# A weight's sign set by the two-slope rectifier, and the last output products of blocks 1 to 4 issued behind the next block's first projections

## The chip, the core and the metric

The kernel runs on one core of a Trainium2 chip. The metric is the time of one execution on the device in microseconds; less is better. The engines that matter are TensorE (PE in the profile, with its weight loads as PEld), VectorE (DVE), ScalarE (ACT), GpSimd (POOL) and SyncE (SP), whose queue issues nearly all transfers between DRAM and on-chip memory.

## What is computed

A causal attention over a window of 64 positions, then a gated MLP with an RMS norm in front of it, then a second MLP. Cut to its core:

```
scores = (q @ k.T) / 8, masked to 0 <= pos_q - pos_k < 64      # 4 x 8 heads, 576 positions, 64 wide
x  = softmax(scores) @ v                                        # rearranged to 2304 tokens x 512
xn = x / sqrt(mean(x*x) + 1e-6) * rms_g
g  = xn @ w_gate                                                # 512 x 1536
x  = (silu(g) * (xn @ w_val)) @ w_out                           # 1536 x 512
h  = x @ w_in2                                                  # 512 x 2048
y  = (h * sigmoid(1.702 * h)) @ w_out2                          # 2048 x 512
```

The MLP weights come as 64-bit floating-point numbers and are needed with more precision than TensorE's fast format holds. Each is turned on the core into two parts, a high one and a remainder, and so is each activation; a product is three matmul terms (high by high, high by remainder, remainder by high).

## The kernel before

The 2304 tokens are six blocks (0 to 5) of 384. The gated MLP runs in two passes over all blocks, six chunks f of 128 hidden units in each pass; the second MLP follows, again over six blocks. The attention of a block is three windows of 128 queries (m = 0 to 17 in all). Windows 0 to 2 are done ahead of everything; the others are woven into pass 0, one block ahead of the block that uses them, so that window 5 is the last that block 1 needs.

**One chunk** (the loop over f): twelve 128x384 matmuls into `psg` (the gate projection), ACT takes the tanh (L623) and DVE makes the gate from it (L626), which frees psg; twelve matmuls into `psv`, DVE multiplies (L630), ACT rounds to `ah` (L633), DVE takes the remainder `al` (L634). Then `emit_O` adds the products of the chunk before with `w_out` into four accumulators acc, again twelve matmuls. psg and psv have one PSUM bank each, so the next psg waits for this chunk's L626 and the next psv for its L630. Behind the last chunk a block has an emit_O without a partner; then the four accumulators are halved into `x2s` tiles (L666 on DVE, L668 on ACT), which have two buffers, and stored (L669).

**The input of a block** is split into `xh` (L423 on ACT, L421 on DVE) and `xl` (L425). A sum of squares on PE (`ps_r`), a power on POOL (L398) and a scaling (L409) stand ahead of that.

**One window of attention**: transposes of k and q, 32 score products `ps_s`, a masked reduction on DVE (L309), the exponential on ACT (L321), a division (L331 to L333), transposes `ps_t` copied out by ACT (L252), 32 value products `ps_v`. The loads of a later window's v wait until an earlier one's has been used.

**A weight step** (`w_step`, L147 on) works on 1024 64-bit words for each partition, as two 32-bit halves `lo` and `hi`: ACT scales `hi` (L163) and `lo` (L164), DVE shifts the exponent bits (L165), sets the sign bit back (L166), and adds `lo` (L169); half a step later ACT rounds (L144) and DVE takes the remainder (L145). There are 34 steps, nine of them in block 0.

**What sets the order.** In pass 0 from block 1 on, the PE instructions stand in program order, and the attention is called at ticks (`score_at`); one tick is one matmul of a projection or of emit_O. PE's order in block 0, and that of the other engines everywhere, is set by a scheduler that models the engines' times when the kernel is built. Between the end of the attention and the second MLP the tile `xr` brings back the first result (L450).

Of the kernel before, what the change touches and what calls it, by code (L numbers as in the profile page):

```python
# [8 lines left out]
F32 = mybir.dt.float32  # L9
F32R = mybir.dt.float32r  # L10
I32 = mybir.dt.int32
U32 = mybir.dt.uint32
AF = mybir.ActivationFunctionType
ALU = mybir.AluOpType
# [8 lines left out]
def window_attention__gated_mlp__mlp_kernel(  # L23
# [13 lines left out]
    nc = tc.nc  # L37
# [4 lines left out]
    KC = DM // 128  # L42
# [6 lines left out]
    TB = 384  # L49
# [8 lines left out]
    stp = ctx.enter_context(tc.tile_pool(name="stp", bufs=3))  # L58
    dram = ctx.enter_context(tc.tile_pool(name="dram", bufs=1, space=bass.MemoryType.DRAM))
    acc_p = ctx.enter_context(tc.tile_pool(name="acc", bufs=1, space=PSUM))  # L60
# [88 lines left out]
    def w_step(limit):  # L149
# [12 lines left out]
        with after(hold[0]):  # L162
            nc.scalar.mul(hi.bitcast(F32), hi.bitcast(F32), 2.0 ** -112)  # L163
            nc.scalar.activation(lo, lo.bitcast(U32), AF.Copy, scale=2.0 ** -29)  # L164
        nc.vector.tensor_scalar(m.bitcast(U32), hi.bitcast(U32), 3, None, ALU.logical_shift_left)  # L165
        nc.vector.scalar_tensor_tensor(  # L166
            m.bitcast(U32), hi.bitcast(U32), 0x80000000, m.bitcast(U32), ALU.bitwise_and, ALU.bitwise_or
        )
# [322 lines left out]
    score_at = [220, 268, 316, 364, 433, 502, 572, 642, 712, 784, 856, 928, 1000]  # L491
# [36 lines left out]
    if True:  # L528
# [49 lines left out]
        T = TB  # L578
        for ps_i in range(2):
            f_lo, f_hi = ps_i * FH, (ps_i + 1) * FH  # L580
            for j in range(NB):
                end = j + 1 == NB
                pinned[0] = ps_i == 0 and j > 0
                acc = [acc_p.tile([128, 512], F32, tag=f"acc{c}", name=f"acc{c}") for c in range(KC)]

                def emit_O(f, ah, al):
# [30 lines left out]
                for f in range(f_lo, f_hi):  # L617
# [24 lines left out]
                    extras(f, 1)  # L642
                    if pend is not None:
                        emit_O(*pend)
# [14 lines left out]
                emit_O(*pend)  # L659
                d = dram.tile([128, KC, TB], F32, name=f"o{ps_i}_{j}", tag=f"o{ps_i}_{j}")  # L660
                for c in range(KC):
                    st = stp.tile([128, TB], F32, tag="os", name="x2s", bufs=2)
                    if ps_i:
                        nc.vector.scalar_tensor_tensor(st, acc[c][:, :T], 0.5, part[:, c, :], ALU.mult, ALU.add)
                    elif c % 2:
                        nc.vector.tensor_scalar(st, acc[c][:, :T], 0.5, None, ALU.mult)  # L666
                    else:
                        nc.scalar.mul(st, acc[c][:, :T], 0.5)  # L668
                    nc.sync.dma_start(out=d[:, c, :], in_=st)  # L669
                (x2d if ps_i else od)[j] = d  # L670
# [86 lines left out]
```

## Time and profile before

| | us |
|---|---|
| median of three runs | 1009.71 |
| range of the runs | 1008.48 to 1009.97 |
| the profiled execution | 1009.22 |
| its span in the profile | 1007.4 |
| PE busy | 976.3 (97%) |
| DVE busy | 514.3 (51%) |
| ACT busy | 407.9 (40%) |

The profiled execution takes 1.8 us more than its span, and lies 0.5 us under the median of the runs. PE is busy nearly always. The stages by time: preparation to 36 us, block 0 to about 100, blocks 1 to 4 with boundaries at about 160, 218, 273 and 329, block 5 to 368, pass 1 to 591, the second MLP to the end.

### The profile page before, as it was taken

The numbers are of one execution on the slowest core, as the hardware profiler recorded it, in microseconds if no ns is written. First come the engines' busy times: TensorE is split into PE (matmuls) and PEld (weight loads), VectorE is DVE, ScalarE is ACT, GpSimd is POOL, SyncE is SP. The second block draws the span as 40 slices with busy tenths as digits, with TensorE's granted clock in tenths as the row PEclk, the third lists the DMA queues.
The fourth block names the chain that finished last, engine by engine and source line by source line (L and its number), as shares of the span: only waits on it lengthen the run. The fifth ranks groups of instructions, "written<-read, shape, count | busy, mean of one in ns | idle before, by whom it ended". The sixth has DMA issues, their size and how long they took to land.

```text
span 1007.4 us, 15580 instructions
## 1 busy us (share of the span) xinstructions
PE 976.3 (97%) x6218; PEld 913.0 (91%) x6218; DVE 514.3 (51%) x1132; ACT 407.9 (40%) x884; POOL 12.6 (1%) x39
## 2 busy tenths in 40 slices
PE   8888998999999999999999999999999999999997
PEld 7888898989988999999999998998999989989996
DVE  5797666576765555564543787242322322322222
ACT  7786655565553333333322464232222322322222
POOL 2000000000000000000000000000000000000000
PEclk9899999999999999999999999999999999999999
DMA  9867455354433431342330441010010100000000
GB/s 225 241 183 198 123 115 159 84 158 116 120 85 122 146 105 43 136 132 88 136 122 15 161 149 57 1 63 1 5 59 1 53 11 1 32 1 1 32 1 32
DMA packets 113321, 88.44 MB, mean 88 GB/s; under 512 B 77664, under 2 KB 104288, under 8 KB 113248
## 3 DMA queue, kind: packets, MB, share of 16 engines
q1 hardware_dynamic: 112720, 87.44, 29.4%
q8 instruction: 49, 0.80, 0.3%
q14 instruction: 24, 0.20, 0.1%
q10 hardware_dynamic: 528, 0.00, 0.0%
HBM read 68.55 MB, written 18.87 MB: 87 GB/s over the span
## 4 chain that ended last, share of the span: by engine, by line
PE 84%; DVE 6%; DMA 4%; ACT 3%; SPq 1%; issue 1%; POOL 0%; ACTq 0%; DVEq 0%
PE acc L684 20%; PE psh L91 20%; PE psg L91 13%; PE psv L91 13%; PE acc L91 12%; PE ps_v L91 1%; PE ps_t L91 1%; SPq L225 1%; PE ps_s L91 1%; DMA st<-in_moe_w_val_dram 1%; PE ps_r L91 1%; DMA o<-x2s 1%; ACT p L321 1%; DVE m L166 1%; DVE xraw L409 1%
## 5 line engine op out<-in xcount | busy, mean ns | idle before, releaser
L700 DVE TENSOR_TENSOR a<-a,psh 128x384 f32<-128x384 f32 x96 | 53.0, 553 | 202.5 <-ACT a L699 202.5
L91 PE MATMUL psh<-x2h,w 128*128 128x384 f32 x768 | 153.2, 339 | 0.2 <-DVE a L700 0.2
L684 PE MATMUL acc<-w,gh 128*128 128x512 f32 x576 | 152.8, 397 | 0.0
L91 PEld LDWEIGHTS psh<-x2h,w 128*128 128x128 f32 x768 | 137.2, 188 | 3.4 <-DVE a L700 0.6
L699 ACT ACTIVATE a<-psh 128x384 f32<-128x384 f32 x96 | 47.2, 492 | 220.5 <-PE psh L91 217.5
L684 PEld LDWEIGHTS acc<-w,gh 128*128 128x128 f32 x576 | 107.0, 188 | 18.5
L91 PE MATMUL acc<-ah,w 128*128 128x384 f32 x576 | 117.2, 341 | 2.5 <-ACT ah L633 2.5
L91 PEld LDWEIGHTS acc<-ah,w 128*128 128x128 f32 x576 | 101.5, 188 | 3.9 <-ACT ah L633 3.2
L91 PE MATMUL psh<-x2l,w 128*128 128x384 f32 x384 | 86.2, 338 | 0.0
L684 PE MATMUL acc<-w,gl 128*128 128x512 f32 x288 | 85.1, 396 | 0.0
L626 DVE SCALAR_TENSOR_TENSOR a<-a,psg 128x384 f32<-128x384 f32 x72 | 39.7, 551 | 88.1 <-ACT a L623 88.1
L704 DVE TENSOR_TENSOR gl<-a,gh 128x384 fp32r<-128x384 f32 x96 | 53.4, 557 | 50.5 <-ACT gh L703 42.7
L623 ACT ACTIVATE a<-psg 128x384 f32<-128x384 f32 x72 | 35.2, 489 | 104.4 <-PE psg L91 104.4
L91 PEld LDWEIGHTS psh<-x2l,w 128*128 128x128 f32 x384 | 69.9, 188 | 5.9
L703 ACT CAST gh<-a 128x384 fp32r<-128x384 f32 x96 | 49.3, 513 | 62.6 <-DVE a L700 49.7
L91 PE MATMUL psg<-xh,w 128*128 128x384 f32 x288 | 66.0, 360 | 8.8 <-DVE a L626 6.2
L633 ACT CAST ah<-a 128x384 fp32r<-128x384 f32 x72 | 37.0, 513 | 75.7 <-DVE a L630 75.5
L684 PEld LDWEIGHTS acc<-w,gl 128*128 128x128 f32 x288 | 54.2, 189 | 12.5
L91 PE MATMUL psv<-xh,w 128*128 128x384 f32 x288 | 64.4, 352 | 0.3 <-DVE a L630 0.3
L91 PE MATMUL acc<-al,w 128*128 128x384 f32 x288 | 63.9, 341 | 0.7 <-DVE al L634 0.7
L91 PEld LDWEIGHTS psg<-xh,w 128*128 128x128 f32 x288 | 52.3, 196 | 13.0 <-DVE a L626 7.3
L321 ACT ACTIVATE p<-p,sm 128x128 f32<-128x128 f32 x128 | 49.7, 393 | 25.5 <-DVE sm L309 25.4
(106 smaller groups left out, 1418.8 us busy)
## 6 DMA issues: line engine op xcount, KB each, us to landing
st<-in_moe_w_out_dram SPq DMA_DIRECT2D x28, 512.0 KB, 4.4
o<-x2s SPq DMA_DIRECT2D x48, 192.0 KB, 2.7
st<-in_moe_w_in_dram SPq DMA_DIRECT2D x16, 512.0 KB, 4.5
st<-in_moe_w_gate_dram SPq DMA_DIRECT2D x12, 512.0 KB, 4.4
st<-in_moe_w_val_dram SPq DMA_DIRECT2D x12, 512.0 KB, 5.5
qkv<-in_v_dram SPq DMA_DIRECT2D x20, 256.0 KB, 3.9
x<-xraw SPq DMA_DIRECT2D x6, 768.0 KB, 3.4
xr<-x SPq DMA_DIRECT2D x6, 768.0 KB, 4.1
```

The source lines that it names most:

```text
L91: ins = op(*args, **kw)
L166: nc.vector.scalar_tensor_tensor(m.bitcast(U32), hi.bitcast(U32), 0x80000000, m.bitcast(U32), ALU.bitwise_and, ALU.bitwise_or)
L225: nc.sync.dma_start(out=t[off:off + n], in_=src[b, :, s:s + n, :].rearrange("h s d -> s h d"))
L321: last_exp[0] = nc.scalar.activation(p[e][:, hp, :], p[e][:, hp, :], AF.Exp, bias=sm[:, 0, i:i + 1], scale=-1.0, accum_out=sm[:, 1, i:i + ...
L623: tanh = nc.scalar.activation(a, psg[:, :T], AF.Tanh, scale=0.5).ins
L626: nc.vector.scalar_tensor_tensor(a, a, 1.0, psg[:, :T], ALU.add, ALU.mult)
L633: ah_ins = nc.scalar.copy(ah, a).ins
L684: nc.tensor.matmul(acc[c], (gh, gh, gl)[pi][:, c * 128:(c + 1) * 128], w[:, (0, 1, 0)[pi], :], start=(f == 0 and pi == 0), stop=(f == NF2 ...
L699: nc.scalar.activation(a[:, :T], psh[:, :T], AF.Sigmoid, scale=1.702)
L700: nc.vector.tensor_tensor(a[:, :T], a[:, :T], psh[:, :T], ALU.mult)
L703: nc.scalar.copy(gh[:, :T], a[:, :T])
L704: nc.vector.tensor_tensor(gl[:, :T], a[:, :T], gh[:, :T].bitcast(F32), ALU.subtract)
```

## The change

Two things change. In a weight step ACT's multiplication by 2^-112 becomes the two-slope rectifier `Prelu`, with a scale of 2^16 and a slope of 2^-32 for negative numbers: a positive number comes out multiplied by 2^16, a negative one by 2^-16, so that a bit of the exponent tells the sign, and the shift by three puts that bit where the sign belongs. The DVE instruction that set the sign (L166 before) is gone. And in pass 0 the last emit_O of blocks 1 to 4, with the halving and the stores behind it, is kept in `late` and called in the next block after the first psg and psv. The next block's accumulators are made after that. The fifth tick is 3 earlier, the sixth 7, and all from the seventh on 12.

```diff
@@ -160,12 +160,9 @@
         else:
             m = tmp.tile([128, 1024], I32, tag="tmp", name="m")
         with after(hold[0]):
-            nc.scalar.mul(hi.bitcast(F32), hi.bitcast(F32), 2.0 ** -112)
+            nc.scalar.activation(hi.bitcast(F32), hi.bitcast(F32), AF.Prelu, scale=2.0 ** 16, alpha=2.0 ** -32)
             nc.scalar.activation(lo, lo.bitcast(U32), AF.Copy, scale=2.0 ** -29)
         nc.vector.tensor_scalar(m.bitcast(U32), hi.bitcast(U32), 3, None, ALU.logical_shift_left)
-        nc.vector.scalar_tensor_tensor(
-            m.bitcast(U32), hi.bitcast(U32), 0x80000000, m.bitcast(U32), ALU.bitwise_and, ALU.bitwise_or
-        )
         nc.vector.tensor_tensor(m, m, lo, ALU.add)
         half.append((pair, m))
         w_load(w_next[1] + 2)
@@ -488,7 +485,7 @@
 
     N_ATT = NG // 2
     m0 = TB // 128
-    score_at = [220, 268, 316, 364, 433, 502, 572, 642, 712, 784, 856, 928, 1000]
+    score_at = [220, 268, 316, 364, 430, 495, 560, 630, 701, 772, 844, 916, 988]
 
     for fn in (att_Tk, att_Tq):
         at_slot(0, 0, lambda fn=fn: held(fn, m0))
@@ -576,14 +573,15 @@
         x_store(0, x)
 
         T = TB
+        late = []
+        part = None
         for ps_i in range(2):
             f_lo, f_hi = ps_i * FH, (ps_i + 1) * FH
             for j in range(NB):
                 end = j + 1 == NB
                 pinned[0] = ps_i == 0 and j > 0
-                acc = [acc_p.tile([128, 512], F32, tag=f"acc{c}", name=f"acc{c}") for c in range(KC)]
-
-                def emit_O(f, ah, al):
+
+                def emit_O(f, ah, al, acc, f_lo=f_lo, f_hi=f_hi):
                     w = weights["o", f]
                     for pi, (wi, aa) in enumerate(((0, ah), (1, ah), (0, al))):
                         for c in range(KC):
@@ -640,8 +638,12 @@
                             split_x(x, nxh, nxl, T)
                         x_store(j + 1, x)
                     extras(f, 1)
+                    if f == f_lo:
+                        if late:
+                            late.pop()()
+                        acc = [acc_p.tile([128, 512], F32, tag=f"acc{c}", name=f"acc{c}") for c in range(KC)]
                     if pend is not None:
-                        emit_O(*pend)
+                        emit_O(*pend, acc)
                     pend = (f, ah, al)
                     extras(f, 2)
                     if f == f_lo:
@@ -656,18 +658,25 @@
                         nc.sync.dma_start(out=part, in_=od[j])
                     if f == f_lo + 3 and (ps_i or end):
                         nxh, nxl = raw_split(0 if end else j + 1, xr)
-                emit_O(*pend)
-                d = dram.tile([128, KC, TB], F32, name=f"o{ps_i}_{j}", tag=f"o{ps_i}_{j}")
-                for c in range(KC):
-                    st = stp.tile([128, TB], F32, tag="os", name="x2s", bufs=2)
-                    if ps_i:
-                        nc.vector.scalar_tensor_tensor(st, acc[c][:, :T], 0.5, part[:, c, :], ALU.mult, ALU.add)
-                    elif c % 2:
-                        nc.vector.tensor_scalar(st, acc[c][:, :T], 0.5, None, ALU.mult)
-                    else:
-                        nc.scalar.mul(st, acc[c][:, :T], 0.5)
-                    nc.sync.dma_start(out=d[:, c, :], in_=st)
-                (x2d if ps_i else od)[j] = d
+
+                def finish(j=j, ps_i=ps_i, pend=pend, acc=acc, emit_O=emit_O, part=part):
+                    emit_O(*pend, acc)
+                    d = dram.tile([128, KC, TB], F32, name=f"o{ps_i}_{j}", tag=f"o{ps_i}_{j}")
+                    for c in range(KC):
+                        st = stp.tile([128, TB], F32, tag="os", name="x2s", bufs=2)
+                        if ps_i:
+                            nc.vector.scalar_tensor_tensor(st, acc[c][:, :T], 0.5, part[:, c, :], ALU.mult, ALU.add)
+                        elif c % 2:
+                            nc.vector.tensor_scalar(st, acc[c][:, :T], 0.5, None, ALU.mult)
+                        else:
+                            nc.scalar.mul(st, acc[c][:, :T], 0.5)
+                        nc.sync.dma_start(out=d[:, c, :], in_=st)
+                    (x2d if ps_i else od)[j] = d
+
+                if ps_i == 0 and 0 < j and not end:
+                    late.append(finish)
+                else:
+                    finish()
                 xh, xl = nxh, nxl
 
         for i in range(NB):
```

**The tail of block 0, on PE.** Before, from the transposes of window 5's probabilities (`ps_t`) on; `ps_v` are its value products, and the acc rows are emit_O of the last two chunks:

```order
L91 MATMUL ps_t<-ident,p 128x128 x8
L91 MATMUL acc_569<-ah,w 128x384
L91 MATMUL acc_570<-ah,w 128x384
L91 MATMUL acc_571<-ah,w 128x384
L91 MATMUL acc_572<-ah,w 128x384
L91 MATMUL acc_569<-al,w 128x384
L91 MATMUL acc_570<-al,w 128x384
L91 MATMUL acc_571<-al,w 128x384
L91 MATMUL acc_572<-al,w 128x384
L91 MATMUL ps_v<-pt,qkv 64x64 x16
L91 MATMUL ps_r<-ones,sq 128x1 x2
L91 MATMUL acc_569<-ah,w 128x384
```

Now, from the end of the last emit_O on; the first `ps_v` row is window 4, the second window 5:

```order
L91 MATMUL acc_681<-al,w 128x384
L91 MATMUL acc_682<-al,w 128x384
L91 MATMUL ps_v<-pt,qkv 64x64 x16
L91 MATMUL ps_t<-ident,p 128x128 x8
L91 MATMUL ps_v<-pt,qkv 64x64 x16
L91 MATMUL ps_r<-ones,sq 128x1 x2
L91 MATMUL ps_k<-ident,qkv 128x128 x4
L91 MATMUL ps_r<-ones,sq 128x1
L91 MATMUL ps_q<-ident,qkv 128x128 x4
L91 MATMUL ps_r<-ident,ry 128x128 x3
L91 MATMUL psg<-xh,w 128x384 x4
```

Window 5's transposes and value products, and window 4's value products too, moved from between the last three emit_O to behind the last one.

**Boundary from block 1 to block 2, on ACT.** Before, from the last chunk's `ah` on; `w` is a weight step's rounding, `x2s` the halving of block 1's accumulators, `p` the exponential of window 9, and the last row the tanh of block 2's first chunk:

```order
L633 CAST ah<-a 128x384
L423 CAST xh<-xraw 128x384 x2
L144 CAST w<-m 128x1024
L252 COPY pt<-ps_t 128x512
L668 ACTIVATE x2s<-acc_1294 128x384
L668 ACTIVATE x2s<-acc_1296 128x384
L321 ACTIVATE p,sm<-p,sm 128x128 x8
L623 ACTIVATE a<-psg 128x384
```

Now, from the same weight step's rounding on, with the tanh of block 2's first two chunks:

```order
L144 CAST w<-m 128x1024
L631 CAST ah<-a 128x384
L420 CAST xh<-xraw 128x384 x2
L318 ACTIVATE p,sm<-p,sm 128x128
L621 ACTIVATE a<-psg 128x384
L318 ACTIVATE p,sm<-p,sm 128x128 x7
L375 ACTIVATE s_2046<-xraw 128x512
L249 COPY KT<-ps_k 128x4x128
L631 CAST ah<-a 128x384
L672 ACTIVATE x2s<-acc_1374 128x384
L249 COPY QT<-ps_q 128x512
L621 ACTIVATE a<-psg 128x384
```

The two halvings moved from ahead of the exponentials and the tanh to behind them (the second stands two rows below the last one shown), and `w` moved from behind the split xh to ahead of ah.

**Boundary from block 4 to block 5, on DVE.** Before; `x2h` and `x2l` are the split of the tile xr, `m` is a weight step, `xh` and `xl` the split of block 5's input:

```order
L630 TENSOR_TENSOR a<-a,psv 128x384
L421 CAST x2h<-xr 128x384
L166 SCALAR_TENSOR_TENSOR m<-st,m 128x1024
L421 CAST x2h<-xr 128x384
L425 TENSOR_TENSOR x2l<-xr,x2h 128x384 x3
L634 TENSOR_TENSOR al<-a,ah 128x384
L421 CAST xh<-xraw 128x384 x2
L425 TENSOR_TENSOR xl<-xraw,xh 128x384
L169 ISA m<-st,m 128x2048
```

Now, from the gate of block 4's last chunk on:

```order
L624 SCALAR_TENSOR_TENSOR a<-a,psg 128x384
L418 CAST x2h<-xr 128x384 x2
L422 TENSOR_TENSOR x2l<-xr,x2h 128x384
L165 TENSOR_SCALAR m<-st 128x1024
L422 TENSOR_TENSOR x2l<-xr,x2h 128x384
L628 TENSOR_TENSOR a<-a,psv 128x384
L166 ISA m<-st,m 128x2048
L422 TENSOR_TENSOR x2l<-xr,x2h 128x384 x2
L632 TENSOR_TENSOR al<-a,ah 128x384
L418 CAST xh<-xraw 128x384 x2
L422 TENSOR_TENSOR xl<-xraw,xh 128x384 x4
```

The last x2l and the step's addition (line 166 now, 169 before) moved from behind the first xl to ahead of al and of the whole split into xh.

## Rows read from the trace of the kernel before

**Rows 1.** Windows: length, busy time (instructions) of PE, PEld, DVE, ACT, POOL, clock, DMA.

```profile
36.00:100.00 64.00, 56.29 (x468) 51.87 (x467) 55.15 (x122) 50.31 (x106) 0.86 (x1) 0.95 0.67 201
...
368.00:591.00 223.00, 223.00 (x1262) 222.56 (x1262) 126.69 (x205) 78.26 (x120) 0.00 (x0) 1.00 0.32 109
```

**Rows 2.** Waits of PE from 36 to 368 us: total us, times, longest.

```profile
PE psg L91 <- DVE a L626: 6.2, 4, 2.2
```

**Rows 3.** Groups by line and shape: busy us, mean ns of one, idle before them.

```profile
L166 DVE SCALAR_TENSOR_TENSOR m<-st,m 128x1024 uint32<-128x1024 uint32 x34 | 41.5, 1221 | 0.4
...
L163 ACT ACTIVATE st<-st 128x1024 f32<-128x1024 f32 x34 | 39.0, 1146 | 10.0 <-DMA st<-in_moe_w_out_dram 5.8 <-DMA st<-in_moe_w_in_dram 3.6 <-DMA st<-in_moe_w_val_dram 0.6
...
L668 ACT ACTIVATE x2s<-acc 128x384 f32<-128x384 f32 x12 | 5.9, 492 | 15.4 <-DMA o<-x2s 8.7 <-PE acc L91 3.0 <-PE ps_q L91 2.4
...
L623 ACT ACTIVATE a<-psg 128x384 f32<-128x384 f32 x72 | 35.2, 489 | 104.4 <-PE psg L91 104.4
```

**Rows 4.** The table load at line 699, on ACT: duration ns, first and last start.

```profile
L699 ACT ACT_TABLE_LOAD  x1: 1283/1283/1283, 597.5 to 597.5; - x1
```

**Rows 5.** Timeline (start us, us, instruction): tail of block 0, first projection of block 1.

```profile
90.17 1.04 PE L91 MATMUL ps_t<-ident,p 128*128 128x128 f32 x8
...
92.67 1.15 PE L91 MATMUL ps_v<-pt,qkv 128*64 128x64 f32 x32
...
94.22 1.66 PE L91 MATMUL acc<-ah,w 128*128 128x384 f32 x8
...
100.58 0.45 PE L91 MATMUL psg<-xh,w 128*128 128x384 f32 x1 [1.25 <-ACT xh L423]
```

**Rows 6.** Timeline, attention window 6: its scores and its division.

```profile
102.99 1.55 PE L91 MATMUL ps_s<-KT,QT 64*64 64x128 f32 x32
...
108.97 1.22 DVE L333 TENSOR_TENSOR p<-p,sm 128x1024 f32<-128x1024 f32 x1
```

**Rows 7.** Page, DMA issues: count, KB each, median us to landing.

```profile
o<-x2s SPq DMA_DIRECT2D x48, 192.0 KB, 2.7
...
qkv<-in_v_dram SPq DMA_DIRECT2D x20, 256.0 KB, 3.9
...
xr<-x SPq DMA_DIRECT2D x6, 768.0 KB, 4.1
```

**Rows 8.** Timeline, boundary from block 1 to block 2.

```profile
158.18 0.45 PE L91 MATMUL acc<-ah,w 128*128 128x384 f32 x1 [1.29 <-ACT ah L633]
...
159.65 1.96 DVE L425 TENSOR_TENSOR xl<-xraw,xh 128x384 fp32r<-128x384 f32 x4
...
165.80 0.49 ACT L668 ACTIVATE x2s<-acc 128x384 f32<-128x384 f32 x1 [4.78 <-DMA o<-x2s]
...
170.38 0.44 PE L91 MATMUL psg<-xh,w 128*128 128x384 f32 x1 [2.15 <-DVE a L626]
```

**Rows 9.** Windows just after two waits: the column behind POOL is the granted clock.

```profile
103.00:107.00 4.00, 4.00 (x41) 3.67 (x41) 3.21 (x20) 2.10 (x11) 0.00 (x0) 0.57 0.48 181
...
172.00:176.00 4.00, 4.00 (x17) 3.97 (x16) 1.57 (x4) 1.00 (x2) 0.00 (x0) 0.60 0.58 100
```

**Rows 10.** Timeline, boundaries from block 2 to 3 and from block 3 to 4.

```profile
227.29 1.68 PE L91 MATMUL psg<-xh,w 128*128 128x384 f32 x8 [1.76 <-DVE a L626]
...
281.99 1.68 PE L91 MATMUL psg<-xh,w 128*128 128x384 f32 x8 [1.31 <-DVE a L626]
```

**Rows 11.** Timeline, boundary from block 4 to block 5.

```profile
317.33 0.34 SPq L450 DMA_DIRECT2D xr<-x  x1
...
321.27 0.87 PE L91 MATMUL acc<-al,w 128*128 128x384 f32 x4
...
321.98 0.93 ACT L423 CAST x2h<-xr 128x384 fp32r<-128x384 f32 x2 [1.41 <-issue]
...
323.38 1.68 PE L91 MATMUL acc<-ah,w 128*128 128x384 f32 x8 [1.23 <-ACT ah L633]
...
329.28 0.91 PE L91 MATMUL psg<-xl,w 128*128 128x384 f32 x3 [0.98 <-DVE xl L425]
```

## The prediction

> **What bounds the kernel now.** I read the page first: PE is busy for 97% of the span, so only PE's idle time can be won. The windows by stage say where it lies. From 368 to 591 us PE is busy for all of 223.00 us, and DVE for 126.69, so a DVE instruction that goes there gives nothing; block 0's stage has 64.00 - 56.29 = 7.7 us without PE [rows 1]. The waits of PE over both stages name what it waits for: most is psg, held until the gate of the chunk before has been made on DVE [rows 2]. The timeline at each boundary then shows why, and the order of the changed kernel shows what stands there now. A change within 0.2%, about 2.0 us, could not be told from none by the measurement of this kernel.
>
> **Part 1, the sign.** One DVE instruction of 1221 ns goes in each of 34 steps, 41.5 us of busy time [rows 3]. ACT's instruction stays one; its price as a rectifier is not in the trace. The multiplication takes 1146 ns, and two functions of one shape, a halving and a tanh, take 492 and 489 ns [rows 3]: so I take no difference for the function, and as bounds 3 ns in 492 either way, under 0.3 us in 34 steps, off PE's path. In pass 1 and later the 1.22 us fall where PE waits for nothing: 0.
>
> In block 0 the relief is real, but the scheduler has spent it on the weights. Nine steps now run ahead of window 4's and window 5's attention, and what was woven between the last output products stands behind them. I work out when window 5 is through. Before, its value products began at 92.67 [rows 5]. By the end of its scores PE will have done all it had done by then except the eight transposes (1.04) and window 4's value products (1.15), which now come later [rows 5]: 92.67 - 1.04 - 1.15 = 90.5, if the waits until then add up to the same. Two chains start there:
> - Window 6 took from the end of its scores, 102.99 + 1.55 = 104.54, to the end of its division, 108.97 + 1.22 = 110.19, so 5.65 us [rows 6]. From 90.5 that is 96.1; transposes of 1.04 and the rest of a copy make it about 97.7.
> - The last emit_O, 8 matmuls in 1.66 and 4 more at the same rate, 2.1 without overlap [rows 5], then window 4's value products, 1.15, end at 93.8. Only then can window 5's v be loaded, 3.9 us to landing [rows 7]: 97.7.
>
> So window 5's value products start at 97.7 instead of 92.67, by either chain. From there to block 1's first projection it was 100.58 - 92.67 = 7.9 us [rows 5]; the last emit_O stood in between and won't now, which may shorten it by 0.9. That gives 104.7 to 105.6, 4.1 to 5.0 later. I take +4.2. Bounds: if waits ahead of the scores vanish, up to 4.2 of the 7.7 us, the term is 0 (below that the later transposes don't let it go); if ACT, which now has a halving of the accumulators ahead of the copies of the transposes, waits there for a store of 2.7 us [rows 7], it is +7. PE will have little to do from 94 to 105. After the wait at 100.58 the clock was 0.57 for 4 us, a mean of its levels 1.2 and 2.4 GHz [rows 9]; I take that as paid either way. The Trainium skill, in "TensorE: Matmul & The Clock Gate" (HAM oscillation), says that an idle stretch sends TensorE back to its slow clock, whose price is then paid once each time. The trace agrees with it here, and by that rule this term keeps its size, since the price was already paid.
>
> **Part 2, the products behind the next projections.** At a boundary PE used to run emit_O twice, then psg; now the second one follows psg and psv. The next block's xh is so needed 2.1 us sooner, and the halvings of the accumulators are made later.
>
> *Block 1 to 2.* Before, PE waited at 158.18 for ah, 1.29 us, and at 170.38 for the gate, 2.15: ACT had stood 4.78 us at the second halving for the store of the first, with the exponentials and the tanh queued behind it [rows 8]. That wait goes, as the halvings now stand behind the tanh. But PE is free for psg at 158.18 - 1.29 = 156.9, and xh is not ready: its ticks have not moved here. Before, xl began at 159.65 with xh complete [rows 8]. One DVE instruction of 1.22 is gone ahead of it, and one as long (L145) is new there, which waits for ACT's rounding; so xh is complete at 159.7 to 160.8, and PE waits 2.8 to 3.9, against 3.4 before. I take 0 (-0.6 to +0.5). The clock of 0.60 after that wait [rows 9] stays too: at the slower level for part of 4 us, about 1.6 us, which a shorter wait would give back at best.
>
> *Block 2 to 3 and 3 to 4.* Waits of 1.76 and 1.31 go [rows 10]: the halvings have left the front of the tanh, and the ticks are 12 matmuls earlier, which is the 2.1 us by which xh is needed sooner. What is late next is the gate of the new first chunk, and scores and emit_O stand ahead of it. I take -1.8 and -1.7, as the value products ahead of them wait a little less too; bounds -2.7 to -0.8 for the first, -2.1 to 0 for the second.
>
> *Block 4 to 5.* Here is no attention left to weave in. Before, the three waits that I count were 1.23 for ah, 0.98 for xl [rows 11] and 0.7 between them, 2.9 in all. Now psg stands directly behind the emit_O that ended at 321.27 + 0.87 = 322.1. xr's load, issued at 317.33 [rows 11], is issued 2.1 sooner and lands after 4.1 [rows 7] at 319.4. Behind it on DVE stand two x2h, four x2l, a shift, the gate product, the step's addition, al and two xh: 0.7 + 2.0 + 0.7 + 0.55 + 1.2 + 0.55 + 0.6 = 6.3, and xh is complete at 325.7. PE waits about 3.7, perhaps with 0.5 for xl: 1.3 more than before. A wait of that length can bring the slower clock, as 2.15 did; before, none followed here. And emit_O of block 5's first chunk may wait for the late halvings, whose stores queue behind weights. I take +1.8, bounds -0.5 and +4.5.
>
> **The sum.** +4.2 + 0 - 1.8 - 1.7 + 1.8 = +2.5 us. On the profiled execution's 1009.22 that is 1011.7; on the median, which lies 0.5 above it, **1012.2 us**.
>
> **The rivals.**
> - *Faster: block 0's tail is not exposed.* If the weights that come sooner let PE lose less before window 5's scores, by 4.2 of the 7.7 us, term 1 is 0 and the sum -1.7; with block 4 to 5 at its lower bound as well it is -4.0, so 1005.7. For it: DVE is busy for most of block 0, and each step is 1.22 shorter. Against it: window 5's chain is now serial, and a gain ahead of it only moves its start. It decides from 93.4 us on: should window 5's value products begin before that, the change is not slower.
> - *No difference.* Term 1 comes out 2 us smaller, or block 4 to 5 costs nothing: -0.2 to +1.0 in sum, 1009.5 to 1010.7.
> - *Worse fronts.* Both fronts without cover, 1 to 2 and 4 to 5, lie at their upper bounds and so does part of the tail: +4.2 + 0.5 - 1.8 - 1.7 + 4.5 = +5.7, 1015.4; with the tail at +6 it is 1017.2.
> - *The rectifier needs another table.* If it were not in the tables that ACT holds, each of 34 steps would load twice, at 1.283 us each [rows 4]: 87 us on ACT, of which 18 steps' share, 46 us, falls into pass 0. Then ACT would be late for the tanh, and block 0 alone, with nine steps and 23 us, would lose most of those: over 1020. Against it: the order shows the same two table loads as before. The Trainium skill, in "ScalarE: Activation LUTs" (What ACT_TABLE_LOAD costs), gives 2.66 us for a switch with its drain, by which it would be 181 us on ACT.
>
> **How the numbers follow.** Forecast, slower by 2 to 5: 0.36. Worse fronts: 0.13. No difference: 0.28. Faster: 0.21. Another table: 0.02. The range takes in the faster rival's end and the worse fronts' first sum with some more: 1005.5 to 1016.5. The chances: slower by over 0.2% 0.51 (the forecast, worse fronts and tables), within 0.2% 0.28, faster by over 0.2% 0.21.
>
> **What would show each step.** Window 5's value products at 97 to 98 and psg of block 1 at 104 to 106, with PE nearly empty between them, show the first term right; a start under 93.4 shows it wrong. At block 1 to 2, a wait for xh near 157 and none for the gate at 168 to 172; at 2 to 3 and 3 to 4, no wait over 0.7 us; at 4 to 5 one wait of 3 to 5 us for xh. All times behind block 0 shift by the first term. The line for the rectifier at 1.1 to 1.2 us, and two table loads, show the price of part 1. Waits in pass 1 or in the second MLP, where PE had none, would make the prediction wrong in a place where I expect nothing.

## The result, and the profile after

The changed kernel takes 1015.35 us (median of four runs, 1014.24 to 1017.12) and the kernel before 1009.1 in the runs beside it (1006.65 to 1009.97): a ratio of 1.0072, with a 95% interval from 1.0055 to 1.0089. It is slower: by 6.2 us by the two medians, and by 7.3 by the ratio, which is the figure used from here on. The two profiled executions differ by 6.0 us of span, 1013.4 against 1007.4. The prediction was 1012.2, in a range of 1005.5 to 1016.5.

Part 1 did to the engines what the diff says. First the head of the page after, then its groups by line (busy us, mean ns of one, idle before them):

```profile
span 1013.4 us, 15582 instructions
PE 982.6 (97%) x6218; PEld 919.9 (91%) x6218; DVE 480.3 (47%) x1098; ACT 409.9 (40%) x884; POOL 12.2 (1%) x39
```

```profile
L163 ACT ACTIVATE st<-st 128x1024 f32<-128x1024 f32 x34 | 38.8, 1140 | 8.0 <-DMA st<-in_moe_w_in_dram 6.7 <-DMA st<-in_moe_w_out_dram 1.4
...
L166 DVE CUSTOM_DVE_ANT_0 m<-st,m 128x2048 uint16<-128x2048 uint16 x34 | 41.5, 1220 | 2.3 <-ACT st L164 1.8
...
L249 ACT ACT_TABLE_LOAD x1 | 1.3, 1283 | 1.3 <-PEq L750 1.3
...
L708 ACT ACT_TABLE_LOAD x1 | 1.3, 1283 | 0.0
```

DVE is busy for 480.3 us instead of 514.3 us; L166 is now the addition, and the sign's 41.5 us [rows 3] are gone. (Elsewhere DVE is busier by 7.5 us; no row here shows where.) The rectifier takes 1140 ns, the multiplication took 1146 [rows 3]. There are two table loads, as before. The Trainium skill says in "ScalarE: Activation LUTs" (Step-by-step: what each stage is for) that each lane takes one element per cycle whatever the function; that the two durations differ by only 6 ns agrees with it.

And pass 1 is unchanged. The window of 223 us that answers to [rows 1], 6 us later:

```profile
374.00:597.00 223.00, 223.00 (x1265) 222.97 (x1264) 113.45 (x191) 80.52 (x122) 0.00 (x0) 1.00 0.34 114
```

So in pass 1 the 13 us less on DVE (113.45 against 126.69) bought nothing, and 6 us were lost ahead of 374 us. They were not lost by more waiting in sum. PE's time without work went from 31.1 us (1007.4 - 976.3) to 30.8 (1013.4 - 982.6), while the same 6218 matmuls kept it busy for 6.3 us longer, at a mean granted clock of 0.981 instead of 0.990. So the waits moved, and TensorE ran longer at the lower clock. Where the waits went, PE's waits over that stretch tell (total us, times, longest), against [rows 2]:

```profile
PE psg L91 <- ACT xh L420: 4.9, 3, 2.3
...
PE ps_v L91 <- issue: 4.5, 2, 2.6
...
PE psg L91 <- DVE xh L418: 2.8, 3, 1.4
...
PE ps_t L91 <- DVE p L330: 2.4, 1, 2.4
...
PE psg L91 <- DVE a L624: 1.5, 1, 1.5
```

The old main wait, psg for the gate, fell from 6.2 us to 1.5. In its place stand waits of psg for xh (4.9 and 2.8) and waits of the value products `ps_v` (4.5), for which the profile names no releaser ("issue"). A table by block says when they cost. The second and third columns are the start of psg of a block's third chunk, from PE's timelines:

| | before | after | later by |
|---|---|---|---|
| block 1, its first psg | 100.58 | 104.98 | 4.4 |
| block 1, third chunk | 118.53 | 123.61 | 5.1 |
| block 2, third chunk | 179.68 | 184.22 | 4.5 |
| block 3, third chunk | 234.63 | 241.94 | 7.3 |
| block 4, third chunk | 289.33 | 296.13 | 6.8 |
| block 5, third chunk | 338.51 | 344.54 | 6.0 |

The rows of blocks 3 and 4 are not quite like for like: ahead of these points the changed kernel has already made 32 score products (at 239.57 for block 3) that came just behind them before (at 235.43), which is 1.0 us of work. Without it these two rows are 6.3 and 5.8. (A row may still be off by some tenths.) So block 0 lost 4.4 us and 0.7 more just after it, the boundary from 1 to 2 gained half a microsecond, 2 to 3 lost 1.8, 3 to 4 gained 0.5, and block 4 with its boundary lost 0.3.

**The tail of block 0.** PE's timeline, to set beside [rows 5]:

```profile
87.42 1.10 PE L91 MATMUL ps_s<-KT,QT 64*64 64x128 f32 x30
...
88.45 1.68 PE L91 MATMUL acc<-ah,w 128*128 128x384 f32 x8
...
90.76 1.15 PE L91 MATMUL ps_v<-pt,qkv 128*64 128x64 f32 x32
...
94.31 1.35 PE L91 MATMUL ps_t<-ident,p 128*128 128x128 f32 x8 [2.39 <-DVE p L330]
...
96.34 1.97 PE L91 MATMUL ps_v<-pt,qkv 128*64 128x64 f32 x30 [0.26 <-ACT pt L249]
...
104.98 0.69 PE L91 MATMUL psg<-xh,w 128*128 128x384 f32 x1 [1.25 <-ACT xh L420]
```

Window 5's scores end at 88.52. The last emit_O (88.45) and window 4's value products (90.76) run, then PE waits 2.39 us for window 5's division, transposes at 94.31, starts the value products at 95.6 (two of them; the rest at 96.34), and reaches block 1 at 104.98.

**The boundary from block 2 to 3.** PE and DVE together:

```profile
218.53 1.10 PE L91 MATMUL ps_s<-KT,QT 64*64 64x128 f32 x32
...
220.19 1.96 DVE L422 TENSOR_TENSOR xl<-xraw,xh 128x384 fp32r<-128x384 f32 x4
...
222.06 1.22 DVE L145 TENSOR_TENSOR w<-m,w 128x1024 fp32r<-128x1024 f32 x1
...
223.20 0.28 DVE L306 CUSTOM_DVE_ANT_0 p<-ps_s,masks 128x128 f32<-128x128 f32 x1
...
223.83 0.29 DVE L306 CUSTOM_DVE_ANT_0 p<-ps_s,masks 128x128 f32<-128x128 f32 x1
...
224.23 1.66 PE L91 MATMUL ps_v<-pt,qkv 128*64 128x64 f32 x32 [2.63 <-issue]
```

The same two rows, scores and first reduction, before:

```profile
216.12 1.10 PE L91 MATMUL ps_s<-KT,QT 64*64 64x128 f32 x32
...
218.76 0.28 DVE L309 CUSTOM_DVE_ANT_0 p<-ps_s,masks 128x128 f32<-128x128 f32 x1
```

PE now makes window 13's scores at 218.53. DVE then has the split of x (220.19 to 222.15) and the remainder of a weight step (L145, 222.06) ahead of the reduction of these scores, which begins at 223.20. The scores lie in the only two PSUM banks that attention has here, four reductions to a bank; the value products need one of them, and start at 224.23, 0.11 us after the end of the fourth reduction (223.83). That is the wait without a name, 2.63 us; at 279.60 there is another of 1.85. The first is followed by a slower clock, which there was none of at this place before; the second is not. Windows of 4 us behind four waits, then windows of 8 us around the last two; the third number from the end is the granted clock:

```profile
107.00:111.00 4.00, 4.00 (x39) 3.33 (x39) 2.70 (x16) 1.00 (x5) 0.00 (x0) 0.50 0.45 178
168.00:172.00 4.00, 4.00 (x46) 3.41 (x48) 2.08 (x17) 1.68 (x8) 0.00 (x0) 0.75 0.02 4
226.00:230.00 4.00, 4.00 (x19) 3.90 (x20) 2.97 (x6) 2.48 (x8) 0.00 (x0) 0.74 0.75 163
331.00:335.00 4.00, 4.00 (x17) 4.00 (x16) 1.34 (x3) 0.49 (x1) 0.00 (x0) 0.64 0.91 344
...
222.00:230.00 8.00, 5.77 (x51) 5.59 (x52) 6.01 (x24) 4.90 (x19) 0.00 (x0) 0.79 0.60 156
...
328.00:336.00 8.00, 6.58 (x28) 6.32 (x29) 4.75 (x11) 1.11 (x3) 0.00 (x0) 0.79 0.71 246
```

Before, two such stretches stood behind these waits in blocks 1 to 5, with 0.57 and 0.60 [rows 9]. Now there are four. The 4-us windows cut the two new ones off at the start; over 8 us, at 0.79, each holds back 8 x 0.21 = 1.7 us of TensorE's time, 3.4 us together.

### The profile page after: what moved, and what is told of

It reads as the page before. It is cut to its first block, busy times and chain, and to the rows that moved or that the text cites. A ratio compares the mean times of both kernels' runs of the same rounds, so it can differ in the third digit from the quotient of the medians.

```text
span 1013.4 us, 15582 instructions
## 1 busy us (share of the span) xinstructions
PE 982.6 (97%) x6218; PEld 919.9 (91%) x6218; DVE 480.3 (47%) x1098; ACT 409.9 (40%) x884; POOL 12.2 (1%) x39
## 4 chain that ended last, share of the span: by engine, by line
PE 88%; DVE 4%; ACT 3%; DMA 3%; issue 1%; POOL 0%; SPq 0%; DVEq 0%; ACTq 0%
PE acc L693 20%; PE psh L91 19%; PE psg L91 14%; PE acc L91 13%; PE psv L91 13%; PE ps_s L91 2%; PE ps_v L91 2%; PE ps_t L91 1%; DMA st<-in_moe_w_in_dram 1%; PE ps_r L91 1%; PE ps_k L91 1%; DVE m L166 1%; ACT quad L318 1%; ACT p L318 1%; PE ps_q L91 1%
## 5 line engine op out<-in xcount | busy, mean ns | idle before, releaser
L91 PE MATMUL psg<-xh,w 128*128 128x384 f32 x288 | 69.9, 370 | 9.2 <-ACT xh L420 4.9
L91 PE MATMUL psv<-xh,w 128*128 128x384 f32 x288 | 62.1, 348 | 0.0
```

The lines of the kernel that those rows point to most:

```text
L91: ins = op(*args, **kw)
```

## The experiments

All times are ratios to the kernel before on the same chip, with 95% intervals; 0.1% is 1.0 us.

| kernel | ratio | interval |
|---|---|---|
| the changed kernel | 1.0072 | 1.0055 to 1.0089 |
| sign alone | 1.0006 | 0.9994 to 1.0017 |
| moved products alone | 0.998 | 0.997 to 0.9989 |
| changed, DVE instruction kept | 0.9965 | 0.9953 to 0.9978 |
| changed, scores of two windows later | 1.0014 | 1.0004 to 1.0024 |
| sign from the tenth step, old place | 0.9947 | 0.9933 to 0.996 |
| changed, old sign in block 0 | 1.0027 | 1.0017 to 1.0038 |
| DVE instruction kept, scores later | 0.9989 | 0.998 to 0.9998 |
| changed, remainder behind | 1.003 | 1.0019 to 1.0042 |
| sign from the tenth step, remainder behind, old place | 0.9908 | 0.9893 to 0.9923 |
| changed, old sign in block 0, remainder behind | 0.9973 | 0.9962 to 0.9985 |
| changed, three blocks late instead of four | 1.0037 | 1.0023 to 1.005 |

### The sign alone

```diff
-            nc.scalar.mul(hi.bitcast(F32), hi.bitcast(F32), 2.0 ** -112)
+            nc.scalar.activation(hi.bitcast(F32), hi.bitcast(F32), AF.Prelu, scale=2.0 ** 16, alpha=2.0 ** -32)
-        nc.vector.scalar_tensor_tensor(m..., 0x80000000, ...)          # in the kernel before
```

> The kernel before with the new sign alone: the rectifier, no sign instruction on DVE, old place of the last output products, old ticks. Theory T (the loss comes from the order of block 0, about 4.4 us at the first psg of block 1 and 0.7 more after it, and only about 1 us from the boundaries): psg of block 1 at 104 to 106 us as in the changed kernel, against 100.6 before; the boundaries keep their waits or lose up to 1.2 us at 158 and 323, where ah waited behind a weight step: 3 to 5 us above before. Rival R (the sign is harmless and the moved products cost it all): psg of block 1 at 99 to 101, time 0 to 2 us below before.

Measured: 0.6 us above before, and no difference by its interval. Block 1's first psg on PE's timeline:

```profile
106.30 0.69 PE L91 MATMUL psg<-xh,w 128*128 128x384 f32 x1 [1.25 <-ACT xh L420]
```

Block 0 loses 5.7 us, and keeps the order of the changed kernel there. But the blocks behind it win all of that back: at block 5's third chunk the kernel is 0.5 us ahead of the one before. Both expectations of the total were wrong: theory T had the loss right and not the gain.

### The moved products alone

```diff
-            nc.scalar.activation(hi..., AF.Prelu, ...)                  # in the changed kernel
+            nc.scalar.mul(hi..., 2.0 ** -112)
+        nc.vector.scalar_tensor_tensor(m..., 0x80000000, ...)
```

> The changed kernel with the old sign (multiplication, and the sign instruction on DVE): the moved products and new ticks alone. Theory T: block 0 as before, psg of block 1 at 100.4 to 100.8; the two waits of the value products that the changed kernel has at 224 (2.6 us) and 280 (1.9 us) stay or grow by up to 1.2 us, since DVE has one instruction more ahead of them: 0 to 3 us above before. Rival R: 4 to 6 us above before.

Measured: 2.0 us below before, which is better than both expectations. Block 0 is as before, psg of block 1 at 100.77. The boundary from 1 to 2 gains 3.0 us in the trace; like for like, the others lie between a loss of 0.7 and a gain of 1.0. The value products' waits are there, but of 1.3 and 1.2 us:

```profile
PE ps_v L91 <- issue: 2.5, 2, 1.3
```

They didn't grow by the instruction more that DVE has, as I had expected; they are about half as long. In this kernel the remainder L145 of the weight step does not stand ahead of the scores' reductions at these two boundaries, and in the changed kernel it does at the first of them. So each half of the change alone does no harm, -2.0 and +0.6 us, and the two together cost 7.3. (The new ticks go with the moved products in every run; the two were not taken apart.)

### The DVE instruction kept

```diff
+        nc.vector.scalar_tensor_tensor(m..., 0x80000000, ...)          # in the changed kernel; sets a bit that is set
```

> The changed kernel with the rectifier, but with the old sign instruction left on DVE as well, where it changes nothing in the data: the same instructions and the same order as the kernel with the old sign and the moved products, only another function on ACT. Theory T: within 0.5 us of that kernel, so the function itself costs nothing, and the 4 to 5 us of block 0 come from the order that the missing DVE instruction brings about. Rival F (the function costs): 1 us or more above it, and the line of the rectifier over 1.2 us.

Measured: 3.5 us below before, 1.5 below the kernel with the moved products alone, and certainly not above it. The order of its instructions is that of the kernel with the moved products alone; only the function on ACT is another. So the rectifier costs nothing, and what costs 10.8 us between this kernel and the changed one is the absence of a DVE instruction, by the order that the scheduler then makes. Of the 1.8 us by which the spans of the two traces with the same order differ, 1.2 are there at block 1's third chunk (117.55 against 118.71): in block 0 the clock fell at another time.

### Scores of windows 13 and 16 later

```diff
-    score_at = [220, 268, 316, 364, 430, 495, 560, 630, 701, 772, 844, 916, 988]
+    score_at = [220, 268, 316, 364, 430, 495, 560, 650, 701, 772, 864, 916, 988]
```

> The changed kernel with the scores of windows 13 and 16 twenty ticks later (650 and 864 instead of 630 and 844), behind the next block's first psg. Theory B (the value products at 224 and 280 wait for a PSUM bank that the scores hold until DVE has done the split of x and a weight's remainder): both waits fall under 0.7 us and the slow clock after the first goes too, 1010 to 1012 us. Rival V (the value products wait for v or for the copied probabilities): the waits stay at 2 us or more, 1014 to 1016 us. Rival X (the split is next): the wait moves to psg of blocks 3 and 4 with 1 to 2 us each, 1012.5 to 1014.

Measured: 1.4 us above before, 5.8 below the changed kernel. Behind block 0 there is no wait for value products left over 0.4 us; block 4's third chunk is 2.4 us later than before instead of 6.8. Its median, 1009.63 us, is slightly better than expected. This run alone doesn't rule out rival V, since the value products are called ten ticks behind the next window's scores and so moved twenty ticks later too. The start times do. In the traces of all these kernels there are 24 waits of over 0.3 us without a name behind block 0, and in each the value products start 0.11 us after the end of the fourth reduction; the copied probabilities had been ready for 4 us or more (218.10 for the products at 224.23). So Theory B holds: the products waited for the bank, and the bank for the reductions.

### The same, with the DVE instruction kept

```diff
-    score_at = [..., 560, 630, 701, 772, 844, 916, 988]                  # in the kernel with the instruction kept
+    score_at = [..., 560, 650, 701, 772, 864, 916, 988]
```

> The kernel with the rectifier, the old sign instruction left on DVE and the moved products (which was 3.5 us below before), and the scores of windows 13 and 16 twenty ticks later. Theory B (value products behind a PSUM bank that scores hold): its two waits of 1.46 us at 215 and 269 go, 5.5 to 7.5 us below before. Rival X (the split of x is next in line): the wait turns up at psg of blocks 3 and 4, 3 to 4.5 us below before.

Measured: 1.1 us below before, 2.4 worse than without the later scores. The two waits of 1.3 us went, and at the same two boundaries psg now waits 0.5 us each for xh, as rival X has it; but the total is outside both expectations. In the traces the two kernels differ by 1.2 us already at block 1's first psg (100.35 against 99.15) and by 1.6 at its third chunk (119.14 against 117.55), where their instructions are the same; that is all of the 1.5 us between their spans. So where the wait was 1.3 us, taking it away gained nothing, and whether it loses anything is open.

### The sign from the tenth step on, old place of the products

```diff
+            if w_next[1] <= n_wh:
+                nc.scalar.mul(hi..., 2.0 ** -112)
+            else:
+                nc.scalar.activation(hi..., AF.Prelu, ...)               # the kernel before otherwise
+        if w_next[1] <= n_wh:
             nc.vector.scalar_tensor_tensor(m..., 0x80000000, ...)
```

> The kernel before with the new sign only from the tenth weight step on: block 0 keeps its old steps and its old order, the last output products stay in their old place. Theory T (the new sign is paid for in block 0 alone, by the order there, and gains at the boundaries where DVE has one instruction less ahead of ah): psg of block 1 at 100 to 101 us, the waits at 158, 170 and 323 smaller, 3.5 to 6.5 us below before. Rival S (the gain that the new sign showed behind block 0 was only a catch-up on time lost in it, such as transfers and steps that were already done when a later block needed them): within 1.5 us of before.

Measured: 5.3 us below before. psg of block 1 at 99.77. Rival S falls, and Theory T holds in the time, but not at each place: at block 1 to 2 the wait for ah grew to 1.78 us, and one of 1.89 for the value products came in place of that for the gate. Only 0.3 us are gained there; in the trace 1.3, 1.8 and 2.1 come at the next three boundaries. So the gain of the new sign behind block 0 is real. It is what I had counted as 0: in blocks 1 to 5 a weight step stands on DVE ahead of ah, of the gate and of the reductions.

### The changed kernel with the old sign in block 0

```diff
+            if w_next[1] <= n_wh: (the old sign)                         # in the changed kernel
+            else: (the rectifier)
```

> The changed kernel with the old sign in block 0's nine weight steps, the new one behind. Theory T: block 0 as before, so 4.5 to 6 us less than the changed kernel, which is 0 to 2.5 us above before: at block 1 to 2 a wait of about 3.5 us for xh, and the value products wait 2 to 3 us at the next two boundaries. Rival S (the boundaries of the changed kernel were worse because block 0 had gone wrong): 2 us or more below before.

Measured: 2.7 us above before and 4.6 below the changed kernel, so block 0's order costs 4.6 us of the 7.3, and the rest is lost behind block 0. The waits of the boundaries are those of the changed kernel:

```profile
PE psg L91 <- ACT xh L427: 5.2, 3, 2.6
...
PE ps_v L91 <- issue: 4.5, 2, 2.6
```

The total came out just above the expected 0 to 2.5. Rival S falls.

### The remainder of the weight step behind

```diff
-        nc.vector.tensor_tensor(w[:, 1, :], w24..., w[:, 0, :]..., ALU.subtract)
+        with after(last_red[0]), after(last_xl[0]):
+            nc.vector.tensor_tensor(w[:, 1, :], w24..., w[:, 0, :]..., ALU.subtract)
```

last_red is the last reduction of scores in blocks 1 and later, last_xl the last xl of a split (L422); the scheduler then puts the rest of the step behind them too.

> The changed kernel with one constraint more: DVE's remainder of a weight step (L145) is issued behind the last split of x and behind the last reduction of scores. Block 0 keeps the changed kernel's order. Theory W (with the sign instruction gone the scheduler pulls the remainder of the step ahead of al, of the split and of the reductions, where it costs more than the instruction saved): at block 1 to 2 the wait for xh falls from 3.5 to under 2 us, the value products' waits fall from 2.8 and 2.0 to under 1.6, 1 to 4 us above before. Rival M (the moved products cost this whatever stands on DVE): waits as in the changed kernel, 6 to 8 us above before.

Measured: 3.0 us above before, 4.2 below the changed kernel. First DVE, ACT and PE at the boundary from 1 to 2 in the changed kernel, then DVE and PE here, where lines are a few numbers higher:

```profile
160.64 1.22 DVE L166 CUSTOM_DVE_ANT_0 m<-st,m 128x2048 uint16<-128x2048 uint16 x1
...
162.46 1.05 ACT L144 CAST w<-m 128x1024 fp32r<-128x1024 f32 x1
...
163.54 1.23 DVE L145 TENSOR_TENSOR w<-m,w 128x1024 fp32r<-128x1024 f32 x1 [1.21 <-ACT w L144]
...
163.82 0.93 ACT L420 CAST xh<-xraw 128x384 fp32r<-128x384 f32 x2
...
164.38 0.45 PE L91 MATMUL psg<-xh,w 128*128 128x384 f32 x1 [2.32 <-ACT xh L420]
...
164.68 0.55 DVE L632 TENSOR_TENSOR al<-a,ah 128x384 fp32r<-128x384 f32 x1
...
165.56 1.76 PE L91 MATMUL psg<-xh,w 128*128 128x384 f32 x7 [0.73 <-DVE xh L418]
```

```profile
161.78 0.56 DVE L639 TENSOR_TENSOR al<-a,ah 128x384 fp32r<-128x384 f32 x1 [0.58 <-ACT ah L638]
...
162.21 1.95 PE L91 MATMUL psg<-xh,w 128*128 128x384 f32 x8
...
162.25 0.62 DVE L425 CAST xh<-xraw 128x384 fp32r<-128x384 f32 x2
...
164.66 1.22 DVE L146 TENSOR_TENSOR w<-m,w 128x1024 fp32r<-128x1024 f32 x1
```

In the changed kernel the whole step runs ahead of al and xh: the addition on DVE (160.64), the rounding on ACT (162.46) and the remainder on DVE (163.54, itself 1.21 us late behind the rounding). psg waits 2.32 us for ACT's part of xh (163.82): it stands behind ah, which the addition and then the rounding hold up. It waits another 0.73 us for DVE's part, which the remainder holds up. Here the whole step is behind, since the scheduler moved the rest with the remainder; al is made at 161.78 and psg starts at 162.21 with no wait for xh. The value products' waits fall to 1.03 and 1.39 us, and one of 1.04 is new. So Theory W holds in time and waits, but at block 1 to 2 the remainder is the smaller part of it. Another wait appears: emit_O waits 2.0 us for the late halvings, once, at block 4 to 5.

### Three blocks late instead of four

```diff
-                if ps_i == 0 and 0 < j and not end:
+                if ps_i == 0 and 0 < j and j + 2 < NB:
                     late.append(finish)
```

> The changed kernel with the last output products of block 4 back in their old place (blocks 1 to 3 stay late). Theory (block 4 to 5 has nothing to cover the wait for xh): the two waits for xh at 328 to 330 (3.1 us) give way to waits for ah and al of 2 to 2.5 us, and the wait of 0.5 us for the late halvings goes, so 1 to 3 us below the changed kernel, 4 to 6 us above before. Rival: the same length, 6 to 8.5 us above before, since the wait for ah takes the place of the one for xh.

Measured: 3.7 us above before, 3.6 below the changed kernel. At the last boundary, in the changed kernel and then here:

```profile
327.85 0.44 PE L91 MATMUL psg<-xh,w 128*128 128x384 f32 x1 [1.35 <-ACT xh L420]
...
329.70 2.01 PE L91 MATMUL psg<-xh,w 128*128 128x384 f32 x7 [1.42 <-DVE xh L418]
...
342.85 1.15 PE L91 MATMUL acc<-ah,w 128*128 128x384 f32 x5 [0.41 <-DVE x2s L670]
```

```profile
328.49 1.68 PE L91 MATMUL acc<-ah,w 128*128 128x384 f32 x8 [0.86 <-ACT ah L631]
...
330.48 0.97 PE L91 MATMUL acc<-al,w 128*128 128x384 f32 x4 [0.32 <-DVE al L632]
```

The waits for xh, 1.35 and 1.42 us, and 0.41 for the halvings give way to 0.86 for ah and 0.32 for al. The rest is clock: the slow stretch behind it doesn't come, and the boundary gains 3.8 us in the trace. The gain is more than the 1 to 3 us that I had expected. (The spans differ by 2.8 only: with the same instructions up to there, this trace is 1.1 us later at block 4's third chunk, behind a longer slow stretch at 224.)

### Both taken back, with and without the moved products

The two edits above together: the new sign from the tenth step on, and the remainder of the step behind. Once in the kernel before, once in the changed kernel.

> The new sign from the tenth weight step on, the old place of the last output products, and the step's remainder (L145) issued behind the last split and the last reduction. Theory W (the remainder pulled ahead of al is what is left of the boundary waits): the wait for ah at 157 (1.9 us) and at 318 (1.35 and 0.7) shrink to under 1 us each, 6.5 to 9 us below before. Rival N (what is left there comes from transfers or from the attention): as the new sign from the tenth step on alone, 4.5 to 6 us below before.

> The changed kernel with the old sign in block 0's nine steps and the step's remainder (L145) behind the last split and the last reduction: the order of block 0 and the pulled remainder both taken back, the moved products and the new ticks kept. Theory T and W together (block 0 costs 4.6 us, the pulled remainder about 4): 1 to 3.5 us below before. If the moved products are worth something in themselves once both are taken back, it is below the kernel with the same two edits and the old place of the products; theory: it is above that one by 3 us or more, since both would remove the same waits.

Measured: 9.2 us below before with the products in their old place, 2.7 below with the products moved. The first is the fastest kernel of this study, 998.71 us, slightly better than Theory W had it, and rival N falls; the second lies in its expected range and 6.5 us above the first. The first kernel's waits of PE, and those of the second:

```profile
PE ps_t L91 <- DVE p L342: 3.7, 2, 3.2
...
PE psg L91 <- DVE a L637: 1.9, 2, 1.0
...
PE acc L91 <- ACT ah L644: 1.1, 1, 1.1
...
PE ps_v L91 <- issue: 0.2, 1, 0.2
```

```profile
PE ps_t L91 <- DVE p L342: 3.9, 2, 2.7
...
PE acc L91 <- ACT x2s L687: 3.7, 3, 2.5
...
PE ps_v L91 <- issue: 3.5, 3, 1.4
...
PE psg L91 <- ACT xh L434: 2.0, 2, 1.2
```

In the first, 3.7 us of waits lie in block 0 and about 3 at the boundaries. In the second the moved products bring 3.7 us of waits for the late halvings, which hold the accumulators, and 3.5 for the value products. So once DVE's weight step is out of the way there is nothing left for the moved products to win, and they cost 6.5 us.

## Why the prediction was right, and where not

The direction was right, and the time lies within the range. The size was not: the sum of +2.5 us, and the 2 to 5 of the likeliest case, were short of the measured 6.0 of span and 7.3 of time. 1015.35 us is nearly the number of the rival "worse fronts" (1015.4), but not for its reasons, so that this is luck: neither front without cover came out at its upper bound. By its steps:

- **Block 0's tail: right in place and mechanism, in size by luck.** +4.2 predicted, 4.4 in the trace. But window 5's scores ended at 88.5, 2 us sooner than the 90.5 that I had reckoned: the weights that came sooner did help ahead of them, as the faster rival had it. So its value products came at 95.6 to 96.3, not at 97 to 98. From there to block 1 it then took 9.4 us, where I had 7.0 to 7.9: new waits of 0.79 and 0.77 us in the sums of squares, and products at a lower clock, 1.97 us for 30 of window 5's value products against 1.15 for all 32 of window 4's. The two misses cancel. The kernel with the old sign in block 0 shows 4.6 us less by time. Not counted were 0.7 us of slower clock behind it: I had taken that price as paid, at 0.57 over 4 us, and from 107 to 111 us it was 0.50, TensorE's level of 1.2 GHz. The Trainium skill, in "TensorE: Matmul & The Clock Gate" (HAM oscillation — how this bites in real kernels), says that an idle stretch sends TensorE back to its slow clock; the trace agrees at this place.
- **The rectifier: right.** No difference by function, and no other table.
- **DVE's relief in pass 1 and later: right where it was read,** 223.00 us busy of 223 in both. What failed is that I priced the relief in blocks 1 to 5 at nothing, but for one instruction at block 1 to 2, by not pricing it at all. There it is worth 5.3 us, as the sign from the tenth step on shows, if the products stay where they were.
- **Block 1 to 2: right.** 0 predicted, 0.5 us gained; the wait for the gate went and one for xh came, of 2.32 and 0.73 us, where I had 2.8 to 3.9 in all. Of its causes I had named the step's remainder; the larger part is the step's addition on DVE and its rounding on ACT, both ahead of ah.
- **Blocks 2 to 3 and 3 to 4: wrong.** -1.8 and -1.7 predicted; like for like the table shows +1.8 and -0.5. The step that failed is "What is late next is the gate of the new first chunk, and scores and emit_O stand ahead of it". I asked what PE's projections wait for and not what the attention woven between them does. The value products wait for a PSUM bank that the scores hold until DVE comes to reduce them. At the first boundary DVE now begins that 4.7 us after the scores (218.53 to 223.20) instead of 2.6 (216.12 to 218.76), with the split of x and the step's remainder ahead of it; at the second, most of the split is ahead of it. Two kernels show it: with the scores later, or the remainder behind, that wait goes or shrinks. So the waits that I had struck out were not gone but moved: 0.59 and 1.76 us before, 2.63 now; 0.42 and 1.31 before, 1.85 now. Most of the 1.8 us is the slow stretch behind the first, which holds back 1.7.
- **Block 4 to 5: right in its place, and nearly in size.** Waits for xh of 2.8 us, where 3.7 had been reckoned, 0.4 for the halvings, and the slower clock that I had put down as possible. Against the boundary with its products back in their old place this costs 3.6 us by time. The +0.3 of block 4 holds also a wait of 1.1 us at 301 for a division that stood there before and is gone, and that I had not looked at; without it the boundary lost 1.3, where +1.8 was predicted, in working that itself came to 1.3.

The largest single thing that the prediction did not see is that the two halves work against each other. The moved products alone are 2.0 us below before, and the sign behind block 0 alone 5.3; the two of them are 2.7 above. Each removes the same waits, DVE's and ACT's lateness at a boundary, so they can't be added; and together they leave a hole on DVE in which the scheduler puts weight work ahead of what PE needs next. The second part is read from the order at the boundaries from 1 to 2 and from 2 to 3, and is borne out by the kernels with the remainder behind.

## What to carry to other kernels

Where a scheduler sets an engine's order from modelled times, an instruction taken away is a new order and not only a shorter one: compare the orders, and look where the freed slot went, before adding up the saving. A wait on a shared buffer, here two PSUM banks, has its price at the reader's place in the queue of another engine, so for each piece of work that is moved ahead ask also whose results lie in the buffers that it will need. When a kernel has become slower, split the loss into time without work and time at a lower clock before explaining it by waits: here PE's time without work was the same. And if two edits remove the same wait, measure them apart: here the smaller edit, used behind block 0 and with one constraint on the order, gave 0.9908, and the larger one only took from it.

## What the runs showed of the hardware

A two-slope rectifier on ACT, with the slope for negative numbers given in the instruction, took 1140 ns for 128x1024 where a multiplication took 1146.

And the clock behind a wait was not a matter of the wait's length alone. Behind single waits of 2.15 us before and of 2.63 after, 4 us at 0.60 and 0.74 followed, while behind 1.76 us [rows 10] and 1.85 us the trace shows none. But two waits in a row at block 4 to 5, of 1.35 and 1.42 us, were followed by 4 us at 0.64 in the changed kernel, while in the kernel with the moved products alone waits of 1.30, 1.41 and 1.13 us at the same boundary were followed by none: its granted clock is 1.00 from 314 to 334 us. Kernels with the same instructions in block 0 differed by 1.2 us there. A difference of one microsecond between two kernels with such waits should not be explained without their clock.
